# A low-rank sum kept in its four groups of partitions, with two copies of V, and another order of the first loads

## The chip, the cores and the metric

The kernel runs on one core of one Trainium2 chip. The metric is the device time of one execution, in microseconds. The kernel before the change took 668.86 us, the median of three runs (668.37, 668.86 and 669.84).

## What is computed

A lightning attention is followed by a mixer with a low-rank token mix. B = 4, H = 8, S = 768, D = 64, so the model width C = H D is 512; the rank is 32.

```python
# attention, in blocks of 64 positions, state kv per (batch, head)
out[block] = ((q @ k.T) * Dmask) @ v + (q * lam_pow) @ kv
kv = lam**64 * kv + (k * rev_pow).T @ v
# mixer: x is out as (B, S, H*D)
h  = x.transpose(0, 2, 1) @ U @ V          # U: 768 x 32, V: 32 x 768
u  = x + h.transpose(0, 2, 1)
ch = relu(u @ w_ch1) @ w_ch2               # 512 x 2048, 2048 x 512
return u + ch
```

U, V, w_ch1 and w_ch2 arrive as 64-bit floats and are turned into 32-bit ones on the chip.

## The kernel before

The 3072 rows (four batches of 768) are worked on as 24 tiles of 128 rows, NT = 6 tiles to a batch. The kernel has two parts. In the first, some 114 us, the attention of all tiles is computed, and the token mix and the split of u into exact pieces follow seven tiles behind. In the second, TensorE multiplies u with w_ch1 and the result with w_ch2, each product as three passes over pieces of the numbers.

**Pieces of numbers.** TensorE multiplies numbers of the type F32R. Where more precision is wanted, a number is split into a high part (its bits under the mask HI) and the rest, its low part, and the products of the parts are summed. For the token mix all four products of V's two parts and of the low-rank sum's two parts are taken.

**The order.** The first part is written out by hand as a list, `pieces` (line 637 and on), of steps per tile s; each engine runs its instructions in the order of that list. For a step s the list has, in short: `prep(s+1)` (q and k of the next tile transposed by TensorE, copied out by ScalarE, L364, and the next loads of q and k issued on SP), `turn` and `mix` of the tiles seven or eight behind, `next_of_low` at a batch's first tile, `scale(s+1)` on GpSimd (qs, ks), `fade` on ScalarE, `split` and `mixed` on VectorE (L628, L629, L571), `intra` and `state` (px and pkv, L447 and L425), `next_v` (the load of v three tiles on, issued on ScalarE's queue), `inter` (L458 and ScalarE's copy x_nat, L464), `scores(s+1)` (pss, L406) and `masked(s+1)` (sm on VectorE, L415). `aside(s)` puts the conversion of U, V and w_ch1 between these, step by step; a conversion's work on ScalarE is put off to `late`.

**The low-rank sum.** After the last tile of a batch, `low(b)` multiplies x of its six tiles with U on TensorE: 48 matmuls, L474. The sum pp is a PSUM tile of 128 x 128: group g of 32 partitions holds columns 128 g to 128 g + 127 of the 32 x 512 result. The tile takes the bank that px uses otherwise. For batches 0 to 2, `low` then copies groups 0 and 1 to rows 0 to 31 of an SBUF tile on ScalarE (L484), and `low_rows` groups 2 and 3 on VectorE (L516), and masks the 32 x 512 result (L519). In the next step three functions, run by `next_of_low`, fill p_hl, 128 x 512: `spread` casts the high part into all four groups (L527: four instructions, 32 x 256), `low_part` subtracts on GpSimd (L531: two, 32 x 256) and `spread_low` copies the low part into the other two groups (L538: two). `mix(s)`, first run one step later, multiplies:

```python
for low in range(2):
    for x in range(2):
        nc.tensor.matmul(out=pm[:, x], lhsT=weights[half[x]],
            rhs=p_hl[half[x], low * 2 * P : (low + 1) * 2 * P], ...)
```

Here half[x] is 64 of the 128 partitions, and `weights` is a slice of v_hl, which holds V's high part in groups 0 and 2 and its low part in groups 1 and 3. The last batch's sum goes another way (one matmul of 128 rows, L566).

**V.** `v_steps` loads V's 64-bit words in two halves, converts them on VectorE and ScalarE, masks them (L700) and fills v_hl: four casts on ScalarE for the high part (L707), two subtractions on VectorE and two on GpSimd for the low part (L711), each 32 x 384.

**Places.** v_hl and p_hl are two parts of one tile `vp` of the weights' pool, and two constants of the conversion (`set_ends`) lie behind them in it. The row of lam has its own small tile.

**First loads.** Before the first step the loads of q, k, q, k (tile 0 in halves) are issued on SP (q) and ScalarE (k), then v, k, v, q on SP (the third k, the first two v, the third q), U, and the fourth k. The third v is issued on ScalarE's queue after `prep(0)`. Every load of q, k or v of a tile is 256 KB in rows of 256 bytes.

Of the kernel before, what the change touches and what calls it, by code (L numbers as in the profile page):

```python
# [14 lines left out]
P = 128  # L15
# [3 lines left out]
def kernel(  # L19
# [267 lines left out]

    assert G == 4
    vp = w1_pool.tile([P, 3, C], F32R, tag="w1", name="vp").rearrange("p n c -> p (n c)")
    v_hl, p_hl = vp[:, 0:S], vp[:, S : S + C]  # L290


    ident = keep.tile([P, P], FP32, name="ident")
    small = consts.tile([P, 16], FP32, name="small")
    zeros = small[:, 0:1]

    mask = consts.tile([P, 2, HP, P], FP32, name="mask")
# [166 lines left out]
        nc.scalar.copy(xs[s].rearrange("p (a x e) -> p x a e", a=HP, x=2), px)  # L464
        del st[s]

    pps, others = {}, {}

    def low(b):

        pp = two_banks("pp", "px")[:, 0, 0:P] if b < B - 1 else bank([P, P], "pp", "b2")
        for c in range(NT):
            for g in range(G):
                nc.tensor.matmul(  # L474
                    out=pp[g * R : (g + 1) * R, :], lhsT=u_w[:, c, :],
                    rhs=xs[b * NT + c][:, g * P : (g + 1) * P],
                    start=(c == 0), stop=(c == NT - 1),
                )
        if b == B - 1:
            pps[b] = pp  # L480
            return
        pps[b] = rows_f = tmp("p_f")[0:R]
        for g in range(2):
            nc.scalar.copy(rows_f[:, g * P : (g + 1) * P], pp[g * R : (g + 1) * R])  # L484
        others[b] = pp

    def low_rows(b):

        pp, t = pps.pop(b), tmp("p_h")[0:R]
        own = [(slice(g * R, (g + 1) * R), slice(g * P, (g + 1) * P)) for g in range(G)]  # L490
        if b == B - 1:
            h, h2, l, l2 = (p_hl[g * R : (g + 1) * R] for g in range(G))
            for rows, cols in own:
                nc.vector.tensor_scalar(
                    t[:, cols].bitcast(U32), pp[rows].bitcast(U32), HI, None, ALU.bitwise_and
                )

            def low_part():
                for rows, cols in own:
                    nc.vector.tensor_tensor(  # L500
                        out=l[:, cols], in0=pp[rows], in1=t[:, cols], op=ALU.subtract
                    )

            def spread():
                nc.scalar.copy(h, t)
                nc.scalar.copy(h2, t)

            def spread_low():
                nc.scalar.copy(l2, l.bitcast(FP32))

            pps[b] = [spread, low_part, spread_low]
            return

        rows_f, pp = pp, others.pop(b)
        for g in range(2, G):
            nc.vector.tensor_copy(  # L516
                out=rows_f[:, g * P : (g + 1) * P], in_=pp[g * R : (g + 1) * R]
            )
        nc.vector.tensor_scalar(t.bitcast(U32), rows_f.bitcast(U32), HI, None, ALU.bitwise_and)  # L519
# [15 lines left out]

        def spread_low():
            for x in range(2):
                nc.scalar.copy(place(2 * x + 1, 1), place(2 * x, 1).bitcast(FP32))  # L538

        pps[b] = [spread, low_part, spread_low]  # L540

    def next_of_low(b):
        pps[b].pop(0)()
# [7 lines left out]

    def mix(s):
        b, c = divmod(s, NT)
        weights = v_hl[:, c * P : (c + 1) * P]
        if b < B - 1:
            pm = both_halves(s)[:, :, 2 * P :]
            for low in range(2):
                for x in range(2):
                    nc.tensor.matmul(  # L559
                        out=pm[:, x], lhsT=weights[half[x]],  # L560
                        rhs=p_hl[half[x], low * 2 * P : (low + 1) * 2 * P],
                        start=(low == 0), stop=(low == 1),
                    )
            return
        pu = bank([P, C], "pu", "b2")
        nc.tensor.matmul(out=pu, lhsT=weights, rhs=p_hl, start=True, stop=True)  # L566
        nc.vector.tensor_tensor(out=xs[s], in0=pu, in1=xs[s], op=ALU.add)

    def mixed(s):
# [64 lines left out]

    splits = {}

    pieces = [("prep", 0), ("third_v", 0), ("scale", 0), ("scores", 0), ("masked", 0)]
    for s in range(NS):
        b, c = divmod(s, NT)
        done = s - NT - 1  # L640
        more = s + 1 < NS
        turns = done > 0 and (done - 1) // TG < FG
        mixes = 0 <= done < NS - NT - 1
        rows = c == 0 and b > 0
        step = [("prep", s + 1)] * more
        step += [("turn", done - 1)] * turns + [("mix", done)] * mixes
        step += [("mix", done + 1)] * (not more)
        step += [("next_of_low", b - 1)] * rows + [("next_of_low", b - 1)] * rows
        step += [("scale", s + 1)] * more
# [12 lines left out]
        step += [("aside", s)] * (0 < s < NT - 2 or s > NT)  # L662
        step += [("masked", s + 1)] * more
        step += [("low_rows", b)] * (more and c == NT - 1)
        step += [("aside", s)] * (s in (0, NT - 2, NT - 1, NT))
        step += [("store", done)] * (done >= 0 and done // TG < FG)
        pieces += step
    waiting = {name: list(range(NS)) for name in "qkv"}

    def load_next(name, engine=nc.sync):  # L670
# [10 lines left out]
        "third_v": lambda s: load_next("v", nc.scalar), "scale": scale, "turned": lambda s: turned.pop(s)(),  # L681
    }
    def v_steps():

# [7 lines left out]
        def parts(gs):  # L692
            for half in range(2):
                rows, cols = slice(half * R, (half + 1) * R), slice(half * SH, (half + 1) * SH)
                for g in gs:
                    yield v_hl[g * R : (g + 1) * R, cols], rows

        def five():
            st["t"] = t = wconv.tile([P, C], FP32, tag="wt", name="vt")[0 : 2 * R, 0:SH]
# [3 lines left out]
            on_scalar(high)  # L703

        def high():
            for out, rows in parts((0, 2)):
                nc.scalar.copy(out, st["t"][rows])  # L707

        def low(g, engine):
            for out, rows in parts((g,)):  # L710
                engine.tensor_tensor(  # L711
                    out=out, in0=st["v"][rows], in1=st["t"][rows], op=ALU.subtract
                )

        halves = [moe_V[:, half * SH : (half + 1) * SH] for half in range(2)]
        return weight_steps(dst, halves, SH, 2 * R, in_parts=True) + [
            five, lambda: low(1, nc.vector), lambda: low(3, nc.gpsimd),
        ]


# [3 lines left out]
    side = {}  # L724
    for steps, at in (
        (u_side, (-1, 1, 1, 2, 2)),
        (v_steps(), (0, 0, 3, 3, 4, 4, 4, 5, 5)),
        (w1_steps(0, True), (3, 4, 5, 6, 8, 9, 10, 11, 13, 14, 15)),
        (w1_steps(1, True, True), (8, 9, 10, 11, 16, 17, 19, 20, 21, 22, 23, NS)),
    ):  # L730
# [14 lines left out]

    ordered = ctx.enter_context(ExitStack())
    ordered.enter_context(tc.manual_schedule())
    lam_row = consts.tile([1, H + P], FP32, name="lam_row")
    blank = x_pool.tile([P, C], FP32, tag="x", name="blank")[:, 0:P]
    nc.vector.memset(blank, 0.0)  # L750
    nc.vector.memset(lam_row[:, H:], 1.0)
    set_ends(vp[:, S + C : S + C + 2].bitcast(FP32))
# [302 lines left out]
```

## Time and profile before

| What | us |
|---|---|
| median of the runs (3) | 668.86 |
| the profiled execution's own time | 665.92 |
| its span | 664.1 |
| TensorE matmuls busy in the span | 655.3 |
| VectorE busy | 491.0 |
| ScalarE busy | 280.2 |
| GpSimd busy | 115.7 |
| end of the attention's last px (L458) | 113.7 |

The span runs from the first to the last instruction that the profile has; times in the profile count from its start. PE is TensorE's matmuls, PEld its weight loads, DVE VectorE, ACT ScalarE, POOL GpSimd, SP SyncE, which only issues transfers here; a q behind a name is the engine's queue. A row of the timeline has start, length, engine, line, operation, out<-in, and in square brackets the idle time of the engine before it with what ended it. TensorE's ends are modelled, so two of its rows can overlap. "issue" is time in which an engine waited for nothing that the profile shows.

### The profile page before, as it was taken

The numbers are of one execution on the slowest core, as the hardware profiler recorded it, in microseconds if no ns is written. First come the engines' busy times: TensorE is split into PE (matmuls) and PEld (weight loads), VectorE is DVE, ScalarE is ACT, GpSimd is POOL, SyncE is SP. The second block draws the span as 40 slices with busy tenths as digits, with TensorE's granted clock in tenths as the row PEclk, the third lists the DMA queues.
The fourth block names the chain that finished last, engine by engine and source line by source line (L and its number), as shares of the span: only waits on it lengthen the run. The fifth ranks groups of instructions, "written<-read, shape, count | busy, mean of one in ns | idle before, by whom it ended". The sixth has DMA issues, their size and how long they took to land.

```text
span 664.1 us, 13400 instructions
## 1 busy us (share of the span) xinstructions
PE 655.3 (99%) x5242; PEld 538.9 (81%) x5242; DVE 491.0 (74%) x862; ACT 280.2 (42%) x530; POOL 115.7 (17%) x98
## 2 busy tenths in 40 slices
PE   8999999999999999999999999999999999999997
PEld 8888989888888888888888888888888888888886
DVE  5579989969999777777796256786685775775854
ACT  4777886555555444444453122332322322322220
POOL 4466876330000000000000000030120300300300
PEclk9999999999999999999999999999999999999999
DMA  9999982445867655555578899763363363543521
GB/s 225 256 239 248 246 216 96 150 169 171 278 239 255 212 201 203 202 202 204 199 267 290 310 324 399 249 211 106 95 209 104 116 192 95 175 141 96 172 82 63
DMA packets 131776, 131.29 MB, mean 198 GB/s; under 512 B 81346, under 2 KB 89794, under 8 KB 131714
## 3 DMA queue, kind: packets, MB, share of 16 engines
q1 hardware_dynamic: 106592, 124.02, 58.3%
q10 hardware_dynamic: 25122, 6.42, 4.3%
q8 instruction: 41, 0.67, 0.4%
q14 instruction: 21, 0.17, 0.1%
HBM read 80.09 MB, written 50.33 MB: 196 GB/s over the span
## 4 chain that ended last, share of the span: by engine, by line
PE 94%; DMA 2%; DVE 1%; SPq 1%; ACT 1%; issue 1%; POOL 0%; ACTq 0%; DVEq 0%
PE pz L818 27%; PE pz L953 14%; PE pz L951 14%; PE pd L828 14%; PE pd L955 13%; PE px L447 3%; PE pss L406 3%; PE px L458 2%; PE pqk L358 2%; PE pkv L425 1%; SPq L279 1%; DMA kraw<-in_k_dram 1%; PE pp L474 1%; DMA qraw<-in_q_dram 1%; PE pm L559 1%; PE put L590 1%
## 5 line engine op out<-in xcount | busy, mean ns | idle before, releaser
L818 PE MATMUL pz<-u_hl,w 128*128 128x512 f32 x768 | 190.1, 398 | 0.0
L818 PEld LDWEIGHTS pz<-u_hl,w 128*128 128x128 f32 x768 | 144.2, 189 | 35.0 <-ACT r L824 0.3
L953 PE MATMUL pz<-w_hl,m 128*128 128x512 f32 x384 | 151.1, 397 | 0.0
L951 PE MATMUL pz<-w_hl,m 128*128 128x512 f32 x384 | 151.0, 397 | 0.0
L955 PE MATMUL pd<-w_d,m 128*128 128x512 f32 x384 | 149.5, 397 | 0.0
L934 ACT ACTIVATE m<-mt 128x512 fp32r<-128x512 f32 x96 | 60.6, 632 | 196.8 <-PE pd L955 137.8
L935 DVE SCALAR_TENSOR_TENSOR m<-rm,m 128x512 fp32r<-128x512 f32 x96 | 71.4, 746 | 52.5 <-ACT m L934 52.2
L980 POOL TENSOR_TENSOR o<-o,u 128x512 f32<-128x512 f32 x20 | 29.8, 1522 | 447.4 <-DVE o L976 447.4
L833 DVE SCALAR_TENSOR_TENSOR r<-pd,r 128x512 f32<-128x512 f32 x96 | 61.8, 686 | 53.3 <-ACT r L824 43.5
L828 PE MATMUL pd<-u_d,w 128*128 128x512 f32 x384 | 98.6, 397 | 0.0
L824 ACT ACTIVATE r<-pz 128x512 f32<-128x512 f32 x96 | 52.1, 596 | 92.7 <-PE pz L818 92.6
L953 PEld LDWEIGHTS pz<-w_hl,m 128*128 128x128 f32 x384 | 72.4, 189 | 17.6
L951 PEld LDWEIGHTS pz<-w_hl,m 128*128 128x128 f32 x384 | 72.4, 188 | 17.6
L955 PEld LDWEIGHTS pd<-w_d,m 128*128 128x128 f32 x384 | 72.4, 189 | 17.5
L828 PEld LDWEIGHTS pd<-u_d,w 128*128 128x128 f32 x384 | 72.2, 189 | 17.2
L936 DVE SCALAR_TENSOR_TENSOR m<-m 128x512 fp32r<-128x512 f32 x96 | 69.0, 721 | 0.9
L933 DVE TENSOR_SCALAR mt<-rm 128x512 uint32<-128x512 uint32 x96 | 46.1, 481 | 28.5 <-DMA rm<-r_d 28.2
L415 DVE TENSOR_TENSOR sm<-pss,mask 128x512 f32<-128x512 f32 x48 | 30.9, 684 | 8.0 <-PE pss L406 7.6
L212 ACT CAST w<-wt 128x512 fp32r<-128x512 f32 x32 | 19.9, 620 | 30.6 <-DVE wt L209 23.4
L447 PE MATMUL px<-vraw,sm 128*64 128x64 f32 x768 | 27.9, 225 | 2.4 <-ACT x_nat L464 0.7
L447 PEld LDWEIGHTS px<-vraw,sm 128*64 128x64 f32 x768 | 25.0, 138 | 5.4 <-ACT qt L364 1.8
L406 PE MATMUL pss<-qt,kt 64*128 64x128 f32 x384 | 28.9, 291 | 0.0
(96 smaller groups left out, 667.7 us busy)
## 6 DMA issues: line engine op xcount, KB each, us to landing
r_d<-r SPq DMA_DIRECT2D x96, 256.0 KB, 2.4
rm<-r_d SPq DMA_DIRECT2D x96, 256.0 KB, 2.7
words<-in_moe_w_ch_dram SPq DMA_DIRECT2D x30, 512.0 KB, 4.4
w_d<-w SPq DMA_DIRECT2D x16, 768.0 KB, 3.4
w_hl<-w_d SPq DMA_DIRECT2D x16, 512.0 KB, 6.3
u_d<-x_nat SPq DMA_DIRECT2D x24, 256.0 KB, 3.9
u<-u_d SPq DMA_DIRECT2D x24, 256.0 KB, 4.1
qraw<-in_q_dram SPq DMA_DIRECT2D x23, 256.0 KB, 4.2
```

The costliest lines, as they stand in the source:

```text
L406: nc.tensor.matmul(out=pss[:, x, a, :], lhsT=kt[half[x], a, :], rhs=qt[half[x], a, :], start=True, stop=True,)
L447: nc.tensor.matmul(out=px[half[t], x, a, :], lhsT=sm[:, x, a, half[t]], rhs=vr[:, 2 * a + x, :], start=(a == 0), stop=(alone and a == HP - 1),
L818: nc.tensor.matmul(out=acc[g][0], lhsT=w[:, n, ct, :], rhs=uhl[g][:, n, ct, :], start=(ct == 0 and n == 0), stop=(ct == CT - 1 and n == 1),)
L824: nc.scalar.mul(rs[g], acc[g][0], 4096.0 + 1.0)
L828: nc.tensor.matmul(out=acc[g][1], lhsT=w[:, 2, ct, :], rhs=ud[g][:, ct, :], start=(ct == 0), stop=(ct == CT - 1),)
L833: nc.vector.scalar_tensor_tensor(rs[g], acc[g][1], 4096.0, rs[g], ALU.mult, ALU.add)
L934: nc.scalar.activation(out=m[:, 0], in_=t, func=AF.Relu)
L935: nc.vector.scalar_tensor_tensor(m[:, 1], r, 0.0, hi, ALU.max, ALU.subtract)
L936: nc.vector.scalar_tensor_tensor(m[:, 2], hi, E, low, ALU.mult, ALU.subtract)
L951: nc.tensor.matmul(out=pz, lhsT=m[:, 0, cols], rhs=hl[:, 0], start=first, stop=False)
L953: nc.tensor.matmul(out=pz, lhsT=m[:, 1, cols], rhs=hl[:, 1], start=False, stop=end)
L955: nc.tensor.matmul(out=pd, lhsT=m[:, 2, cols], rhs=dd, start=first, stop=end)
```

## The change

The low-rank sum stays in its four groups. VectorE copies the whole 128 x 128 tile to SBUF and masks it there; ScalarE casts each group's high part (four, 32 x 128), and GpSimd subtracts each group's low part (four, 32 x 128), into a p_hl of 128 x 256. A half x of its partitions holds, in its first 32, the high part of columns 256 x to 256 x + 255, and in its second 32 their low part. The four products then need V twice: once with its high part in groups 0 and 2 and its low part in 1 and 3, and once the other way round. v_hl becomes 128 x 2 x 768. The conversion fills only group 0 (high, ScalarE) and group 1 (low, GpSimd) of the first copy, and six transfers inside SBUF, 32 x 768 each, issued on SP at the start of step 6 (`spread_v`), fill the other six places. The first mix is in step 7.

Each mix is still four matmuls over 64 partitions and 256 columns. The last batch's four parts lie in the second copy of V, which is no longer needed then.

v_hl fills `vp`; p_hl becomes a tile of its own, the row of lam moves into the tile of `blank` (zeros), and the two constants into `small`.

In the first loads, v, k, v, q becomes v, k, q, k; U comes after that. The second v is issued on ScalarE's queue after `prep(0)` and the third after `prep(1)`.

```diff
-    v_hl, p_hl = vp[:, 0:S], vp[:, S : S + C]
+    v_hl = vp.rearrange("p (n c) -> p n c", n=2)
+    p_hl = consts.tile([P, 2 * P], F32R, name="p_hl")
...
     def low(b):
...
-        pps[b] = rows_f = tmp("p_f")[0:R]
-        for g in range(2):
-            nc.scalar.copy(rows_f[:, g * P : (g + 1) * P], pp[g * R : (g + 1) * R])
-        others[b] = pp
+        pps[b] = pp
...
     def low_rows(b):
...
-        rows_f, pp = pp, others.pop(b)
-        for g in range(2, G):
-            nc.vector.tensor_copy(
-                out=rows_f[:, g * P : (g + 1) * P], in_=pp[g * R : (g + 1) * R]
-            )
-        nc.vector.tensor_scalar(t.bitcast(U32), rows_f.bitcast(U32), HI, None, ALU.bitwise_and)
-        wide = [slice(x * 2 * P, (x + 1) * 2 * P) for x in range(2)]
+        whole, t = tmp("p_f")[:, 0:P], tmp("p_h")[:, 0:P]
+        nc.vector.tensor_copy(out=whole, in_=pp)
+        nc.vector.tensor_scalar(t.bitcast(U32), whole.bitcast(U32), HI, None, ALU.bitwise_and)
 
         def place(g, low):
-            return p_hl[g * R : (g + 1) * R, wide[low]]
-
-        def spread():
+            n = 2 * (g // 2) + low
+            return p_hl[n * R : (n + 1) * R, (g % 2) * P : (g % 2 + 1) * P]
+
+        def high_part():
             for g in range(G):
-                nc.scalar.copy(place(g, 0), t[:, wide[g // 2]])
+                nc.scalar.copy(place(g, 0), t[g * R : (g + 1) * R])
 
         def low_part():
-            for x in range(2):
+            for g in range(G):
+                rows = slice(g * R, (g + 1) * R)
                 nc.gpsimd.tensor_tensor(
-                    out=place(2 * x, 1), in0=rows_f[:, wide[x]], in1=t[:, wide[x]],
-                    op=ALU.subtract,
-                )
-
-        def spread_low():
-            for x in range(2):
-                nc.scalar.copy(place(2 * x + 1, 1), place(2 * x, 1).bitcast(FP32))
-
-        pps[b] = [spread, low_part, spread_low]
+                    out=place(g, 1), in0=whole[rows], in1=t[rows], op=ALU.subtract
+                )
+
+        pps[b] = [high_part, low_part]
...
     def mix(s):
-        weights = v_hl[:, c * P : (c + 1) * P]
+        weights = v_hl[:, :, c * P : (c + 1) * P]
...
-            for low in range(2):
+            for n in range(2):
                 for x in range(2):
                     nc.tensor.matmul(
-                        out=pm[:, x], lhsT=weights[half[x]],
-                        rhs=p_hl[half[x], low * 2 * P : (low + 1) * 2 * P],
-                        start=(low == 0), stop=(low == 1),
+                        out=pm[:, x], lhsT=weights[half[x], n], rhs=p_hl[half[x]],
+                        start=(n == 0), stop=(n == 1),
                     )
...
-        step = [("prep", s + 1)] * more
-        step += [("turn", done - 1)] * turns + [("mix", done)] * mixes
+        step = [("spread_v", s)] * (s == NT) + [("prep", s + 1)] * more
+        step += [("another_v", s)] * (s == 0) + [("turn", done - 1)] * turns + [("mix", done)] * mixes
...
-        step += [("next_of_low", b - 1)] * rows
...
     def v_steps():
...
-            for out, rows in parts((0, 2)):
+            for out, rows in parts(0):
                 nc.scalar.copy(out, st["t"][rows])
 
-        def low(g, engine):
-            for out, rows in parts((g,)):
-                engine.tensor_tensor(
+        def low():
+            for out, rows in parts(1):
+                nc.gpsimd.tensor_tensor(
                     out=out, in0=st["v"][rows], in1=st["t"][rows], op=ALU.subtract
                 )
 
+        def spread():
+            whole = v_hl.bitcast(FP32)
+            for g, n in ((2, 0), (1, 1), (3, 1), (3, 0), (0, 1), (2, 1)):
+                source = (g + n) % 2
+                nc.sync.dma_start(
+                    out=whole[g * R : (g + 1) * R, n],
+                    in_=whole[source * R : (source + 1) * R, 0],
+                )
...
-    for name in "vkvq":
+    for name in "vkqk":
         load_next(name)
     aside(-1)
-    load_next("k")
```

More of the change, by code (lines that the diff above doesn't have):

```diff
@@ L289 @@
     vp = w1_pool.tile([P, 3, C], F32R, tag="w1", name="vp").rearrange("p n c -> p (n c)")
-    v_hl, p_hl = vp[:, 0:S], vp[:, S : S + C]
+    v_hl = vp.rearrange("p (n c) -> p n c", n=2)
+    p_hl = consts.tile([P, 2 * P], F32R, name="p_hl")
     ident = keep.tile([P, P], FP32, name="ident")
-    small = consts.tile([P, 16], FP32, name="small")
+    small = consts.tile([P, 18], FP32, name="small")
     zeros = small[:, 0:1]
@@ L465, in inter @@
         del st[s]
-    pps, others = {}, {}
+    pps = {}
     def low(b):
@@ L481, in low @@
             return
-        pps[b] = rows_f = tmp("p_f")[0:R]
-        for g in range(2):
-            nc.scalar.copy(rows_f[:, g * P : (g + 1) * P], pp[g * R : (g + 1) * R])
-        others[b] = pp
+        pps[b] = pp
     def low_rows(b):
-        pp, t = pps.pop(b), tmp("p_h")[0:R]
+        pp = pps.pop(b)
         own = [(slice(g * R, (g + 1) * R), slice(g * P, (g + 1) * P)) for g in range(G)]
         if b == B - 1:
-            h, h2, l, l2 = (p_hl[g * R : (g + 1) * R] for g in range(G))
+            t = tmp("p_h")[0:R]
+            h, h2, l, l2 = (v_hl[g * R : (g + 1) * R, 1, 0:C] for g in range(G))
             for rows, cols in own:
@@ L565, in mix @@
         pu = bank([P, C], "pu", "b2")
-        nc.tensor.matmul(out=pu, lhsT=weights, rhs=p_hl, start=True, stop=True)
+        nc.tensor.matmul(out=pu, lhsT=weights[:, 0], rhs=v_hl[:, 1, 0:C], start=True, stop=True)
         nc.vector.tensor_tensor(out=xs[s], in0=pu, in1=xs[s], op=ALU.add)
@@ L635 @@
     splits = {}
-    pieces = [("prep", 0), ("third_v", 0), ("scale", 0), ("scores", 0), ("masked", 0)]
+    pieces = [("prep", 0), ("another_v", 0), ("scale", 0), ("scores", 0), ("masked", 0)]
     for s in range(NS):
@@ L679 @@
         "mixed": mixed, "store": store, "next_v": next_v, "split": lambda s: splits.pop(s)(),
-        "third_v": lambda s: load_next("v", nc.scalar), "scale": scale, "turned": lambda s: turned.pop(s)(),
+        "another_v": lambda s: load_next("v", nc.scalar), "scale": scale, "turned": lambda s: turned.pop(s)(),
     }
@@ L690, in dst, with parts @@
             return st["v"]
-        def parts(gs):
+        def parts(g):
             for half in range(2):
                 rows, cols = slice(half * R, (half + 1) * R), slice(half * SH, (half + 1) * SH)
-                for g in gs:
-                    yield v_hl[g * R : (g + 1) * R, cols], rows
+                yield v_hl[g * R : (g + 1) * R, 0, cols], rows
         def five():
@@ L705, in high @@
         def high():
-            for out, rows in parts((0, 2)):
+            for out, rows in parts(0):
                 nc.scalar.copy(out, st["t"][rows])
-        def low(g, engine):
-            for out, rows in parts((g,)):
-                engine.tensor_tensor(
+        def low():
+            for out, rows in parts(1):
+                nc.gpsimd.tensor_tensor(
                     out=out, in0=st["v"][rows], in1=st["t"][rows], op=ALU.subtract
                 )
+        def spread():
[6 more added lines that the diff above has]
+                )
+        run["spread_v"] = lambda s: spread()
         halves = [moe_V[:, half * SH : (half + 1) * SH] for half in range(2)]
         return weight_steps(dst, halves, SH, 2 * R, in_parts=True) + [
-            five, lambda: low(1, nc.vector), lambda: low(3, nc.gpsimd),
+            five, low,
         ]
@@ L726 @@
         (u_side, (-1, 1, 1, 2, 2)),
-        (v_steps(), (0, 0, 3, 3, 4, 4, 4, 5, 5)),
+        (v_steps(), (0, 0, 3, 3, 4, 4, 4, 5)),
         (w1_steps(0, True), (3, 4, 5, 6, 8, 9, 10, 11, 13, 14, 15)),
@@ L747 @@
     ordered.enter_context(tc.manual_schedule())
-    lam_row = consts.tile([1, H + P], FP32, name="lam_row")
-    blank = x_pool.tile([P, C], FP32, tag="x", name="blank")[:, 0:P]
+    blank = x_pool.tile([P, C], FP32, tag="x", name="blank")
+    lam_row, blank = blank[0:1, P : P + H + P], blank[:, 0:P]
     nc.vector.memset(blank, 0.0)
     nc.vector.memset(lam_row[:, H:], 1.0)
-    set_ends(vp[:, S + C : S + C + 2].bitcast(FP32))
+    set_ends(small[:, 16:18])
     nc.scalar.dma_start(out=lam_row[:, 0:H], in_=lam.unsqueeze(0))
```

## The prediction

> **What bounds the kernel now.** I read the engine shares first, then busy time by stretches, then the chain that ended last, then the timeline wherever that chain leaves TensorE. In the busy times by stretch the first four numbers after the width are TensorE's matmuls, its weight loads, VectorE and ScalarE:
>
> ```profile
> 0.00:30.00 30.00, 26.83 (x588) 24.40 (x588) 16.90 (x46) 16.50 (x41) 14.23 (x18) 1.00 1.03 235
> 30.00:60.00 30.00, 28.86 (x794) 26.33 (x796) 24.56 (x44) 22.52 (x54) 19.50 (x17) 1.00 1.03 251
> 60.00:90.00 30.00, 29.50 (x824) 27.03 (x822) 27.16 (x47) 23.01 (x55) 22.16 (x19) 1.00 0.97 244
> 140.00:400.00 260.00, 260.00 (x1111) 209.14 (x1110) 192.95 (x346) 117.64 (x204) 2.60 (x2) 1.00 0.68 236
> ```
>
> From 115 us on TensorE has no gap until the last stores. So a microsecond won before that should reach the end whole, and only some 5 us can be won: 3.2, 1.1 and 0.5 us idle in these stretches and 0.3 up to 115. The change touches four places there. The first is in the timeline:
>
> ```profile
> 12.33 0.47 PE L358 MATMUL pqk<-ident,qraw 64*128 64x64 f32 x8 [0.91 <-DMA qraw<-in_q_dram]
> ```
>
> The third q arrives at 12.19 and TensorE has waited 0.91 us. The second place is the first use of the low-rank product, in the chain (start, length, what):
>
> ```profile
> 38.60 0.49 PE pqk L358 x16
> 39.09 0.18 PE pm L559 x2
> 39.27 0.39 ACT vp L538
> 39.66 0.02 issue
> 39.69 0.59 ACT x_nat L464
> 40.28 0.04 issue
> 40.33 1.15 PE px L447 x32
> ```
>
> ScalarE is late. The four copies of V (L707, 2.07 us), two of the product (L484, 0.52), four of its high part (L527, 1.66) and two of its low part (L538, 0.83) stand in its queue between 32.5 and 39.7, and the evacuation L464 that frees the px bank is behind them. The other two places are the next batch boundaries, alike:
>
> ```profile
> 62.26 0.67 PE pqk L358 x16
> 62.92 0.01 issue
> 62.94 0.28 DVE p_f L516
> 63.22 0.01 issue
> 63.24 0.30 DVE p_f L516
> 63.54 0.02 issue
> 63.56 0.41 DVE p_h L519
> 63.98 0.03 issue
> 64.01 0.70 DVE ut L628
> 64.71 0.02 issue
> 64.73 0.69 DVE u_hl L629
> ```
>
> Here the product occupies the px bank until VectorE's second copy ends (63.54), and px starts at 63.63. The VectorE row that follows (ut, u_hl, x_nat, kv) ends at 66.36, and the next pqk shares kv's bank.
>
> **What the skill says.** *DMA: Bandwidth & Descriptors*, "Issuing engines are not separate DMA queues": SP and ScalarE feed the same 16 DMA engines. The trace agrees: a DMA share of 1.03 with both queues in use. So moving v to ScalarE's queue reorders the loads; it makes no bandwidth. The same page, "Anatomy of one DMA", has about 2.0 us fixed cost per transfer, mostly the write's receipt, fitted on another path. The shortest landing of a q load here is 2.4 us, so I use 2.0 as the floor for the new copies. *SBUF — State Buffer*, "SBUF: two separate sides", has an exclusive lock between VectorE (two SBUF inputs) and GpSimd. The trace agrees: L531 takes 1.02 us beside VectorE's L711 and 0.72 without it.
>
> **The change, part by part.**
>
> *Matrix products.* Eighteen mixes of four matmuls, [64 x 128] by 256 columns, before and after. 0.
>
> *Product rows (low, low_rows, three boundaries).* Removed from each: ScalarE 2 x 0.256 (L484) + 4 x 0.403 (L527) + 2 x 0.403 (L538) = 2.93 us. Added: four casts 32x128. The casts take 403, 510 and 618 ns for 256, 384 and 512 columns, so 0.84 ns a column and 296 ns for 128: 1.18 us. ScalarE saves 1.75 us. VectorE drops 2 x 0.288 + 0.414 and gains one 128x128 copy from PSUM (0.288, the row of equal width) and one mask of 128 columns (192 columns take 0.25, 384 take 0.35, so 0.22): it saves 0.48 us and no longer waits for ScalarE's two copies. GpSimd: two at 0.726 become four; 512 columns take 1.28, so 2.16 ns a column and 0.45 us each: +0.35 us. This is covered: its qs is used 2.1 us after it is ready (67.02 against 69.14). Without that cover it would be 0.35 us a boundary.
>
> At 62.26: copy to 62.6, mask to 62.85, ut from the turn's end at 63.2 instead of 64.01. The px bank is free at 62.6, so px follows the mix after 0.41 us, as in other steps, not 0.66: 0.25. From pss to pqk it is 0.99 us in other steps and 1.23 here (65.18 to 66.41): 0.24. Kv then ends near 65.7, before pqk wants its bank at 65.9. Gain 0.49; at the third boundary 0.19 + 0.24 = 0.43. Together 0.9 us.
>
> *V's parts.* VectorE loses 2 x 0.767, ScalarE 2 x 0.51. GpSimd keeps two at 1.0 us. In their place SP issues six copies inside SBUF, 32 rows x 3 KB, at the head of step 6, past the loads of q and k behind them. SP is free then: its next load waits for TensorE from 33.5 to 35.73. The first copies wait for ScalarE's two casts (33.55) and the others for GpSimd (34.26). But the trace has eight semaphores for transfers, used about in turn, and an issue waits until the transfer before it on its semaphore has landed. If the six take them in turn, the fifth waits for a q load that landed at 35.37 and the sixth for a k load at 37.04. The DMA engines were nearly idle then:
>
> ```profile
> 36.00:37.00 1.00, 1.00 (x38) 1.00 (x40) 0.95 (x3) 0.95 (x2) 0.65 (x1) 1.00 0.24 66
> ```
>
> So the first five flow at once, and the sixth lands at about 37.1 + 2.0 = 39.1. No row shows such a copy. From below: no semaphore wait, all landed by 38, before the mix at 38.9 needs them. From above: 6.4 us, the longest landing of a k load in this trace, so 43.5. I take 39.1: the engines have little else to do. The last matmul of the mix then ends near 39.4 and px starts at 39.45 instead of 40.33: gain 0.9. With no late copy it is px at 39.3 (the mix's 0.41 after 38.89): 1.0. With 43.5 it is a loss of 3.5. ScalarE has x_nat done by 39.0 and doesn't decide. The q, k and weight loads behind the six come about 1.5 us later; q of tile 10 lands by 42.5 and is read at 47. V's load on ScalarE stays ahead of x_nat. If its semaphore were the sixth copy's, x_nat would end at 39.8 and 0.4 of the gain would go.
>
> *Order of the first loads.* Third q takes the second v's place in SP's queue (landed 11.29), the second v takes the third v's on ScalarE (issued 6.36, landed 10.71), and the third v goes after the second tile's copies, at about 9.4. TensorE is ready for q at 11.42, so up to 0.9 us is won there; the second v is needed at 12.1. But the bytes up to the fourth q are the same set, at 235 GB/s and full engines, and it landed at 15.95 with TensorE ready at 16.05. At 21 us DMA decides once more: ScalarE's issue of the sixth v (21.13) waits for the semaphore of a k load that lands at 21.05, and the x_nat of tile 2 is queued behind it. I expect 0.3 us to be left at 22 us. What is left only brings TensorE earlier to the mix, which waits for the sixth copy: 0 to 0.9 from below and above, taken as 0.
>
> *Small moves* (lam_row into blank's tile, ends into small, k's fourth load ahead of U): no instruction more, a few load places; 0.
>
> **Sum.** 0.9 (first mix) + 0.9 (two boundaries) + 0 = 1.8 us. The profiled execution ran 665.92 us with a span of 664.1, so it would be 664.1 with a span of 662.3. It lies 2.9 below the median of the runs, 668.86, and I take the difference off that: 667.1. A measurement of this kernel can tell about 0.2%, 1.3 us, from no change.
>
> **Rivals.**
> (1) All cover holds: the copies land before the mix wants them and 0.9 of the order of loads survives. 1.0 + 0.9 + 0.9 = 2.8, so 666.1. For it: the DMA gap at 36 us. Against it: full DMA engines until 35.
> (2) The copies or a semaphore wait on ScalarE eat the gain at the first mix, and only the boundaries are left: 0.9, so 668.0, within 0.2%. For it: each of the six is one more link in SP's order.
> (3) Slower: the sixth copy lands late. One place, the mix of tile 0. It decides once the landing passes 42.3 (px then at 42.6, 2.3 us lost against 0.9 won). At 43.5, with px at 43.8, it costs 3.5 - 0.9 = 2.6: 671.5. For it: landings of 5.2 us in the middle and 6.4 at most on the same queue. Against it: those were in full queues.
> (4) The load order does nothing, since DMA is full: already in my sum.
>
> **How the numbers follow.** Forecast 0.42, (1) 0.13, (2) 0.31 with shifts to zero or a little above, (3) 0.14, of which 0.02 stays inside 0.2%. Faster 0.55, same 0.33, slower 0.12. The range, 665.7 to 669.9, holds (1), the forecast and (2) with the spread of the runs (about 0.7 either side), and leaves out most of (3). The forecast's own range is 666.4 to 667.6.
>
> **What would show it.** L484 and L538 gone; px of tile 7 at 39.3 to 39.8; pqk 0.99 us after pss at both later boundaries; six SBUF copies on SP between 33.5 and 37.5, the last landing near 39; no wait of TensorE for q at 12 us. I am wrong if the mix of tile 0 waits for a DMA beyond 40, if a ScalarE load waits for a copy's semaphore, or if GpSimd's four subtractions end after the next mix wants them.

## The result and the profile after

The changed kernel took 670.78 us, the median of seven runs (669.61 to 672.07). The kernel before, run beside it, took 669.15 (666.65 to 670.21). The ratio is 1.0031, with a 95% interval of 1.0015 to 1.0047: slower by 1 to 3 us, where 1.8 us less was forecast. The profiled execution ran 669.61 us with a span of 667.7; that of before ran 665.92 with 664.1.

The busy times by stretch after the change, in the columns of before (start and end, width, TensorE's matmuls, weight loads, VectorE, ScalarE, GpSimd, granted clock, DMA share, GB/s):

```profile
0.00:30.00 30.00, 27.78 (x595) 25.40 (x596) 17.07 (x46) 16.51 (x41) 14.21 (x18) 1.00 1.05 239
30.00:60.00 30.00, 28.17 (x724) 25.69 (x720) 20.25 (x37) 18.89 (x46) 17.53 (x18) 0.94 0.97 241
...
```

From 60 us on the clock is 1.00 as before. In the first stretch TensorE is busy 0.95 us longer than before. ScalarE, at 22.52 us in the second, is down to 18.89, in part simply because the stretch holds less of the work (724 matmuls where it held 794). The new number is the clock of the second stretch: 0.94, where it was 1.00. A slower clock makes TensorE busier for the same work, so the matmul column alone hides it.

TensorE's timeline at the first use of the product, tile 0's mix in step 7:

```profile
38.03 0.36 PE L551 MATMUL pm<-p_hl,vp 64*128 64x256 f32 x1
38.90 0.35 PE L551 MATMUL pm<-p_hl,vp 64*128 64x256 f32 x1 [0.51 <-ACT qt L365]
40.45 0.53 PE L551 MATMUL pm<-p_hl,vp 64*128 64x256 f32 x2 [1.20 <-DMA vp<-vp]
40.90 1.52 PE L448 MATMUL px<-vraw,sm 128*64 128x64 f32 x32
```

The mix could start at 38.03, but its matmuls come one by one, as the copies land, and the last two only at 40.45. (The profile puts the second one's wait down to ScalarE's qt, which the mix does not read; that matmul needs the fourth copy, which landed at 38.65.) So px starts at 40.90; it was 40.33 before, and 39.45 was forecast. TensorE does almost nothing for 2.2 us. And px then takes 1.52 us for the work that took 1.15 before.

Why it takes longer stands in the columns of the same view by single microseconds:

```profile
39.00:40.00 1.00, 0.25 (x1) 0.05 (x1) 0.07 (x1) 0.97 (x4) 1.00 (x2) 1.00 0.68 209
40.00:41.00 1.00, 0.56 (x4) 0.46 (x6) 0.00 (x0) 0.48 (x3) 0.49 (x1) 1.00 1.07 243
41.00:42.00 1.00, 1.00 (x29) 1.00 (x31) 0.69 (x1) 0.00 (x0) 0.00 (x0) 0.75 1.11 260
42.00:43.00 1.00, 1.00 (x24) 1.00 (x22) 0.00 (x0) 0.00 (x0) 0.00 (x0) 0.50 0.91 227
43.00:44.00 1.00, 1.00 (x34) 0.88 (x34) 0.42 (x1) 0.00 (x0) 0.64 (x1) 0.50 1.24 289
44.00:45.00 1.00, 1.00 (x23) 0.88 (x17) 0.00 (x0) 0.59 (x1) 0.42 (x1) 0.55 1.08 287
```

The column after GpSimd is the granted clock. It falls to one half in the 42nd microsecond and comes back in the 45th: 0.25 + 0.5 + 0.5 + 0.45 = 1.7 us of clock lost, or 3.4 us at half speed. The chain that ended last shows what stands ahead of it:

```profile
30.51 6.37 DMA kraw<-in_k_dram
36.88 0.01 issue
36.90 3.42 DMA vp<-vp
40.31 0.14 issue
40.45 0.53 PE pm L551 x2
40.97 1.45 PE px L448 x32
```

The load of k that was issued at 30.51 lands at 36.88 and releases the issue of a copy, which takes 3.42 us to land; and that copy is the fifth, not the sixth. All six, as one group of instructions (nanoseconds of an issue, least, middle and most; first and last start; then the time from issue to landing, of the five copies whose landing can be told):

```profile
L708 SPq DMA_DIRECT2D vp<-vp x6: 537/589/659, 33.7 to 37.6; - x6
DMA to landing us min/median/max: 2.9/3.3/3.7
```

The sixth is issued at 37.60 and lands at 40.48.

At the third batch boundary the row that holds the px bank is one copy of 128x128 and one mask of 128 columns, as worked out:

```profile
92.10 0.29 DVE L514 COPY p_f<-pp 128x128 f32<-128x128 f32 x1 [0.18 <-PE pp L475]
92.50 0.23 DVE L515 TENSOR_SCALAR p_h<-p_f 128x128 uint32<-128x128 uint32 x1
...
93.35 2.00 POOL L528 TENSOR_TENSOR p_hl<-p_f,p_h 32x128 fp32r<-32x128 f32 x4 [1.20 <-PE pm L551]
```

px (93.15) follows the mix (92.74) after 0.41 us. I compare the steps by the times at which the scores (pss) of a tile start on TensorE:

| Start of the scores of tile | 7 | 9 | 12 | 14 | 18 | 20 | 23 | end of span |
|---|---|---|---|---|---|---|---|---|
| before | 37.43 | 46.84 | 59.65 | 69.77 | 86.91 | 96.97 | 109.88 | 664.1 |
| after | 36.57 | 48.86 | 61.80 | 72.26 | 89.42 | 99.12 | 112.94 | 667.7 |

The changed kernel is 0.86 us ahead at tile 7 and 2.02 behind at tile 9: 2.9 us went in two steps. The 0.86 is mostly not the change's work: 0.52 of it is a pause in the execution of before, at 35.43, that the profile puts down to "issue". The third boundary (18 to 20) takes 9.70 us in place of 10.06. The second (12 to 14) takes 10.46 in place of 10.12, with a pause of 0.67 us in its px that the profile puts down to "issue". Between tiles 20 and 23 another 0.91 us is lost, which I did not settle. From tile 23 to the end it is 554.8 in place of 554.2. That last half microsecond and the pauses are taken up below.

### The profile page after: what moved, and what is told of

Read it like the earlier page. It is cut to its first block, busy times and chain, and to the rows that moved or that the text cites. A ratio compares the mean times of both kernels' runs of the same rounds, so it can differ in the third digit from the quotient of the medians.

```text
span 667.7 us, 13403 instructions
## 1 busy us (share of the span) xinstructions
PE 658.0 (99%) x5242; PEld 541.1 (81%) x5242; DVE 488.1 (73%) x857; ACT 273.9 (41%) x516; POOL 116.0 (17%) x104
## 4 chain that ended last, share of the span: by engine, by line
PE 97%; DMA 1%; issue 0%; ACT 0%; SPq 0%; DVE 0%; DVEq 0%; ACTq 0%
PE pz L816 27%; PE pz L951 13%; PE pd L826 13%; PE pz L949 13%; PE pd L953 13%; PE pss L407 4%; PE px L448 4%; PE px L459 2%; PE pqk L359 2%; PE pkv L426 2%; DMA kraw<-in_k_dram 1%; PE pm L551 1%; PE pp L475 1%; PE pm L599 1%; PE put L581 1%; DMA vp<-vp 1%
```

## The experiments

The theory I formed from these lines: the copies land late, TensorE idles, its clock is halved for 3.4 us, and these two together are the loss. The rivals: the new order of the first loads, the number of copies in SP's queue, or something later in the run. Experiments of one batch share a chip and the runs of the kernel before, so the 667.07, 666.84 and 666.88 below are three such batches. The diffs are shortened.

**TensorE kept busy while it waits.** Eight matmuls on zeros (their result is used by nothing) stand ahead of tile 0's mix:

```diff
+        step += [("busy", s)] * (s == NT + 1)      # keep_busy(8)
         step += [("turn", done - 1)] * turns + [("mix", done)] * mixes
```

> The changed kernel, with eight matmuls on zeros (128 x 128, result unused) ahead of the mix of tile 0, so that TensorE works while it would wait for the copies of V. Theory A (the late copies stall TensorE, and the idle time lets its granted clock fall to half): px of tile 7 starts where it does in the changed kernel (41.0 us, within 0.4), the granted clock stays at 1.00 from 41 to 45 us, and the run is 1.2 to 1.8 us shorter than the changed kernel: ratio to before 1.000 to 1.001. Rival B (the new order of the first loads costs the time): nothing changes, ratio 1.002 to 1.004. Rival C (the fall of the clock has another cause than the idle time): clock and ratio as in the changed kernel.

Measured: 668.14 us (14 runs) against 667.07; ratio 1.0008, interval 0.9990 to 1.0026. TensorE's timeline of this kernel:

```profile
37.73 2.05 PE L344 MATMUL idle<-blank 128*128 128x128 f32 x16
41.03 0.72 PE L551 MATMUL pm<-p_hl,vp 64*128 64x256 f32 x3 [0.75 <-DMA vp<-vp]
41.68 1.15 PE L448 MATMUL px<-vraw,sm 128*64 128x64 f32 x32
```

(The eight matmuls are 16 instructions in the trace.) Here the copies landed even later, the last at 41.26, and px starts at 41.68, later than expected (41.0, to within 0.4). But it takes 1.15 us, the clock is 1.00 in every microsecond from 41 to 45, and all 14 runs have a mean clock of 0.998 or more. From this px to the scores of tile 9 it is 6.47 us; in the kernel before it is 6.51 and in the changed one 7.96. So the halved clock costs 1.45 us where it happens, and keeping TensorE at work removes it although the copies are no earlier. The trace shows this, the times do not: the changed kernel was not run in this batch, and the interval here overlaps those of its two measurements (1.0015 to 1.0047 above, 1.0010 to 1.0041 below).

**One copy instead of six.** The engines fill two groups of both copies of V, and one transfer of 64 partitions fills the rest (one more pair of casts on ScalarE, one more pair of subtractions, on VectorE):

```diff
-            for g, n in ((2, 0), (1, 1), (3, 1), (3, 0), (0, 1), (2, 1)):
-                source = (g + n) % 2
-                nc.sync.dma_start(out=whole[g * R : (g + 1) * R, n], in_=whole[source * R : (source + 1) * R, 0])
+            nc.sync.dma_start(out=whole[2 * R :], in_=whole[0 : 2 * R])
```

> The changed kernel with the first two groups of both copies of V filled by the engines (ScalarE four casts instead of two, VectorE two subtractions more, GpSimd two as it was) and one transfer of 64 partitions by 6 KB in place of the six. Theory A: it is issued by 34.5 us and lands by 38.2, px of tile 7 starts at 38.3 to 39.2 instead of 41.0, the clock stays at 1.00, and the run is 3 to 4 us shorter than the changed kernel: ratio to before 0.996 to 0.999. Rival B: px of tile 7 earlier, but a ratio of 1.002 or more. If this copy lands only at 40, the clock falls again and the ratio stays near 1.003.

Measured: 667.20 us (22 runs) against 667.07; ratio 0.9996, interval 0.9982 to 1.0010. The single copy is issued at 34.98 and lands at 39.74, after 4.8 us; 38.2 was expected:

```profile
39.88 0.47 PE L551 MATMUL pm<-p_hl,vp 64*128 64x256 f32 x3 [1.71 <-DMA vp<-vp]
40.27 1.29 PE L448 MATMUL px<-vraw,sm 128*64 128x64 f32 x32
```

In this execution the clock fell as well (0.57 to 0.50 from 41 to 44), and from px to the scores of tile 9 it is again 7.96 us. The runs differ: the four with a mean clock of 0.997 took 668.5 us in the middle (one with 0.996 took 669.6), the six with 0.998 took 667.6, and the five with 0.999 and the six with 1.000 took 666.0 and 667.0. So one copy does not always escape the drop. The time met neither expectation: not the 0.996 to 0.999 of a copy that lands by 38.2, nor the 1.003 of one that lands at 40.

**The load order alone**, in the kernel before:

```diff
-    for name in "vkvq":
+    for name in "vkqk":
         load_next(name)
     aside(-1)
-    load_next("k")
...
+        step += [("third_v", s)] * (s == 0)        # load_next("v") on ScalarE's queue
```

> The kernel before with the new order of the first loads alone (v, k, q, k on SP; second and third v on ScalarE's queue). Theory A: TensorE's wait for q at 12 us goes, scores of tile 3 start up to 0.3 us earlier, and little is left: ratio 0.9985 to 1.0005. Rival B: ratio 1.002 to 1.004.

Measured: 666.83 us (22 runs) against 667.07; ratio 0.9993, interval 0.9981 to 1.0005. No loss, and no gain that can be told. TensorE's wait for q at 12 us is gone, but the scores of tile 3 start at 19.43, where it was 19.40.

**The changed kernel with the old load order:**

```diff
-    for name in "vkqk":
+    for name in "vkvq":
         load_next(name)
     aside(-1)
+    load_next("k")
...
-        step += [("another_v", s)] * (s == 0)
```

> The changed kernel with the order of the first loads as before the change. Theory A: the sixth copy still lands after 40 us, TensorE waits and its clock falls; ratio to before 1.002 to 1.004. Rival B: the loss is gone, ratio 0.997 to 1.000.

Measured: 668.95 us (22 runs) against 667.07; ratio 1.0028, interval 1.0013 to 1.0043. As slow as the changed kernel. In its profiled execution the whole chain is later: copies issued from 36.32 to 40.22, the last landing at 42.66, and TensorE's wait longer:

```profile
42.54 0.81 PE L551 MATMUL pm<-p_hl,vp 64*128 64x256 f32 x3 [2.90 <-DMA vp<-vp]
```

Its clock falls at 41.48 and stays at one half for 6.8 us, twice as long as in the changed kernel. The wait alone costs time too: the seven runs with a mean clock of 0.999 or 1.000 took 668.6 us in the middle. So the order of the loads is not the cause of the loss.

**The first mix later in its step.** If the copies' lateness is all, TensorE should be given other work until they land. Tile 0's mix goes behind the second px of tile 7, and what VectorE does with its result goes behind with it:

```diff
-        ... [("mix", done)] * mixes
+        ... [("mix", done)] * (mixes and done > 0)
...
         step += [("next_v", s), ("inter", s)]
+        step += [("mix", done)] * (done == 0)
...
-        step += [("mixed", done)] * mixes
+        step += [("mixed", done)] * (mixes and done > 0)
...
         step += [("low", b)] * (more and c == NT - 1)
+        step += [("mixed", done)] * (done == 0)
```

> The changed kernel with the mix of tile 0 put later in the step, behind inter(7) and ahead of scores(8), so that TensorE has px, pkv and the second px of tile 7 to do while the copies land. Late copies and the clock that falls behind them as the cause: the copies land near 40.5 and the mix wants them near 41, TensorE is not idle for 2 us, the granted clock stays at 1.00 from 41 to 45, px of tile 7 starts at 38.3 to 39.2, and the kernel is 3 to 3.8 us shorter than the changed kernel: ratio to before 0.996 to 0.999. If the loss comes from something later in the run: ratio 1.001 to 1.004, as the changed kernel.

Measured: 664.60 us (8 runs) against 666.84; ratio 0.9966, interval 0.9951 to 0.9980. The timeline of this kernel:

```profile
38.66 1.24 PE L448 MATMUL px<-vraw,sm 128*64 128x64 f32 x32 [0.35 <-issue]
40.92 0.51 PE L551 MATMUL pm<-p_hl,vp 64*128 64x256 f32 x4
41.26 1.05 PE L407 MATMUL pss<-qt,kt 64*128 64x128 f32 x16
```

The copies land no earlier (the last at 40.78), but the mix wants them at 40.92, only just later: its four matmuls run in one row with no wait, px has already run at 38.66, and the clock is 1.00 from 37 to 46. The scores of tile 9 start at 45.45, 1.39 us earlier than in the kernel before and 3.41 earlier than in the changed one. (Of the 1.39, 0.77 were there at the scores of tile 7 already, mostly the pause in the execution of before.) The changed kernel, run in the same batch, took 668.81 us, and no run of it was as short as the longest of these eight.

**The later mix with the product's rows gathered as before** (two copies each on ScalarE and VectorE into 32 partitions, a mask of 512 columns, then two casts and two subtractions of 256 columns into the new p_hl):

```diff
-        whole, t = tmp("p_f")[:, 0:P], tmp("p_h")[:, 0:P]
-        nc.vector.tensor_copy(out=whole, in_=pp)
+        for g in range(2): nc.scalar.copy(rows_f[:, g * P : (g + 1) * P], pp[g * R : (g + 1) * R])
+        for g in range(2, G): nc.vector.tensor_copy(out=rows_f[:, g * P : (g + 1) * P], in_=pp[g * R : (g + 1) * R])
...
-            for g in range(G): nc.scalar.copy(place(g, 0), t[g * R : (g + 1) * R])
+            for x in range(2): nc.scalar.copy(place(x, 0), t[:, wide[x]])
```

> The same, with the low-rank product's rows gathered in 32 partitions as before the change (ScalarE two and VectorE two copies, a mask of 512 columns, two casts of 256 columns, two subtractions on GpSimd of 256 columns). If the gain at the two batch boundaries belongs to the split in four groups: each boundary 0.36 to 0.44 us longer than in the kernel with the later mix, 0.8 us over the whole, ratio 0.001 above that one. If the gain has another cause: the same time as that one.

Measured: 666.25 us (14 runs), ratio 0.9998, interval 0.9982 to 1.0015. The boundaries give the cleaner reading: the second takes 10.12 us and the third 10.06, exactly as in the kernel before, and 9.69 each with the split in four groups. That part of the change is worth 0.43 + 0.37 = 0.80 us. The medians stand 1.65 us apart, which their intervals allow but the boundaries do not explain.

**The kernel before with the same later mix** (the same diff):

> The kernel before, with the mix of tile 0 put later in the same way. If ScalarE's lateness at the first mix is what the later place removes, px of tile 7 starts at 39.3 instead of 40.33 and the kernel gains up to 1.0 us: ratio 0.9985 to 1. If the gain of the later place needs the change: ratio 1.

Measured: 667.34 us (14 runs), ratio 1.0014, interval 1.0000 to 1.0028.

```profile
39.44 1.15 PE L447 MATMUL px<-vraw,sm 128*64 128x64 f32 x32 [1.18 <-ACT x_nat L464]
```

px starts at 39.44, near the 39.3 that was expected, but not for the expected reason: this execution was 0.83 us ahead at the scores of tile 7 (36.60 against 37.43). Counted from there px comes after 2.84 us, where it was 2.90, because it still waits for ScalarE, which has its four casts for V and the product's copies in its queue; and the mix now comes behind it, so the scores of tile 8 come after 5.45 us, where it was 5.12. The later place alone gains nothing. That what it uses is the room on ScalarE that the change makes fits this wait, but was not tested apart.

**The changed kernel again**, on the same chip:

> The changed kernel itself, to be compared on the same chip: ratio 1.002 to 1.004, granted clock 0.995 to 0.997 in every run, px of tile 7 near 40.9 and the clock at half for some 3 us after it.

Measured: 668.81 us (10 runs) against 666.84; ratio 1.0025, interval 1.0010 to 1.0041. The expectation had the clock drop in every run. It was in seven, with a mean clock of 0.996 or 0.997 and 668.6 to 669.3 us in the middle. Three had 0.999: two of them took 666.2 and 666.6, no more than the kernel before, the third 668.8; and one of the seven took 667.05. So the time goes with the clock, by some 2 us, but not run by run, and the clock does not always fall. In the profiled execution it falls at 40.64, for 3.4 us again, and px starts at 41.22. There the fourth copy is the late one: its issue took 1.82 us and it landed at 40.10. (The profile puts TensorE's wait of 2.01 us down to GpSimd's qs, which the mix does not read.) In six of the eight traces with six copies one of the issues took 1.2 to 1.8 us; what held it is not shown.

**Two transfers more.** The last half microsecond: in the kernels with six copies the span ends 3.3 us after VectorE's last operation, in those without copies 2.8. SP's last instructions wait in a fixed order for eight transfer semaphores. In the kernel before the last two stores are on semaphores 105 and 106, second and third in that order. With six more transfers they are on 102 and 104, the last store on the one that is asked for first; all other waits then follow its landing, and in each such trace there is a pause of some 0.3 us between two of them. So I split two later loads in halves, which makes the six transfers more into eight:

```diff
-            nc.sync.dma_start(out=us[n], in_=u_d[g * TG + n])
+            halves = [slice(0, C // 2), slice(C // 2, C)] if g == 0 and n < 2 else [slice(0, C)]
+            for part in halves:
+                nc.sync.dma_start(out=us[n][:, part], in_=u_d[g * TG + n][:, part])
```

> The kernel with the later mix, with two loads of the second part (u of tiles 0 and 1 of the first group) split in halves, so that the program has eight transfers more than the kernel before instead of six. In all six kernels profiled with the six copies the span ends 3.3 us after VectorE's last operation, in the three without them 2.8: the last stores' semaphores come first instead of third in SP's closing row of waits. If that is the cause: the stores are back on the semaphores they have in the kernel before, and the span ends 2.8 to 2.9 us after VectorE's last operation, 0.5 us shorter than with the later mix alone (too little for the times alone: ratio to before about 0.996 against 0.9966). If the 0.5 us belongs to the copies in another way: 3.3 us as with the later mix.

The timeline's head and VectorE's last operation in this kernel:

```profile
core 0 of [0], span 662.3 us
...
658.61 0.75 DVE L978 SCALAR_TENSOR_TENSOR o<-pd,o 128x256 f32<-128x256 f32 x2
```

From 659.36 to 662.3 it is 2.9 us; with the later mix alone it was 3.3 (658.77 to 662.1). So 0.4 us is back, with the stores again on 105 and 106. The order of the waits is not all of it: the kernel with one copy, whose stores are on 106 and 107, has 3.4, with the same pause behind the waits; why the pause comes is not shown. The time, 665.25 us (9 runs) against 666.88, ratio 0.9977, interval 0.9959 to 0.9996, is too coarse to show that.

**One copy, later mix and two split loads** together:

> The kernel with one copy of 64 partitions instead of six of 32 (the engines fill two groups of both copies of V), with the later mix, and the two split loads. If a copy that lands before the mix wants it costs nothing, and the six copies cost nothing beyond that either: the copy lands near 39.7, the mix starts near 41 without a wait, clock 1.00, and the time is that of the kernel with the later mix within 1 us, ratio 0.995 to 0.998. If SP's four us of issues held up the loads behind them: 0.5 to 1 us shorter than the kernel with the later mix and two more transfers. Both stores at the end on later semaphores: span ends 2.6 to 3.0 us after VectorE's last operation.

Measured: 665.61 us (14 runs), ratio 0.9980, interval 0.9966 to 0.9994. The copy is issued at 36.19 in this execution and lands at 40.90; the mix starts at 42.30 without a wait. The last stores are on 108 and 109, and the span ends 3.0 us after VectorE's last operation, as expected. It is no faster than six copies: once the mix does not wait for them, SP's four us of issues cost nothing that can be told.

**The later mix once more**, beside the last two:

> The kernel with the later mix again, to be compared on the same chip: ratio 0.995 to 0.998, granted clock 0.998 to 1, span ending 3.3 us after VectorE's last operation.

Measured: 665.64 us (22 runs) against 666.88; ratio 0.9979, interval 0.9970 to 0.9989, every run with a clock of 0.998 or more. By its two measurements the kernel with the later mix beats the kernel before by 0.2 to 0.3%, and the changed one by 0.6% in the batch that has both.

One step of all traces, side by side, free of what each execution gained or lost before it:

| From the scores of tile 7 to those of tile 9 | us |
|---|---|
| before | 9.41 |
| before, new load order | 9.41 |
| before, later mix | 10.03 |
| changed (two traces) | 12.29, 12.39 |
| changed, TensorE kept busy | 12.01 |
| changed, old load order | 14.13 |
| changed, one copy | 11.89 |
| later mix (two traces) | 8.79, 8.93 |
| later mix, rows gathered | 8.80 |
| later mix, two transfers more | 8.79 |
| later mix, one copy | 9.14 |

## Why the prediction was wrong, step by step

**The first mix (forecast: gain 0.9; it lost 2.0 in the trace).** Two steps failed.

The first is "the sixth lands at about 37.1 + 2.0 = 39.1". The mechanism was there: an issue held until a k load landed at 36.88. Three terms were short. The load's semaphore held the fifth copy, since a load of v had taken a turn between, so a whole issue followed. An issue takes 0.54 to 0.66 us, and I had given it nothing. And a landing takes 2.9 to 3.7 us. The 2.0 us of the Trainium skill (*DMA: Bandwidth & Descriptors*, "Anatomy of one DMA") was fitted on another path; I used it as a floor and then took the floor for the value, since the engines were "nearly idle". That held for one microsecond, 36 to 37; the next two of the trace of before have a DMA share of 1.04 and 1.20. How much of a landing is the queue's and how much the copy's own is not shown: the first of the six, too, took 3.7 us. The sum is 37.60 + 2.88 = 40.48. For px that is 1.45 us, 40.90 in place of 39.45. This is rival (3)'s mechanism at less than its size.

The second is rival (3)'s point of decision: "once the landing passes 42.3". It priced each us of TensorE's wait at one us. By that price px at 40.90 is 0.57 us worse than before, which the boundaries pay for, and the kernel would still have been a little faster. The halved clock added 1.45 us, and neither a step nor a rival had it. The Trainium skill has the effect: *TensorE: Matmul & The Clock Gate*, "What's actually happening", gives half the clock after an idle window of about 3.4 us, and full clock after about as long at work. The second number is what this trace shows (3.4 us at half). The first is not: here the clock fell after 3.4 us in which TensorE was busy for half of the time. The same section calls the window free-running, and the traces agree: the clock changes only on a grid of 3.41 us that does not follow the waits (last section). That in the three runs with a mean clock of 0.999 the pause lay across two stretches of the grid would fit; none of them was profiled.

**The two boundaries (forecast 0.49 + 0.43).** Right: 0.43 and 0.37 by the kernel with the rows gathered again. The prices behind them were right too: copy 0.29 (0.288), mask 0.23 (0.22), cast 0.296 (0.296), GpSimd 0.45 each (0.45). In the changed kernel's own trace the second boundary shows no gain because of the 0.67 us "issue" pause. Such pauses of 0.3 to 1.6 us stand at other places in each execution, that of before included. What causes them stays open.

**The order of the first loads (forecast: 0.3 us ahead at 22 us, worth nothing).** That it is worth nothing was right: alone it changes nothing that can be told. In the two traces TensorE is 0.33 us ahead at the scores of tile 6 (31.58 against 31.91), but over all traces that time lies anywhere from 30.68 to 32.52, with either order, so the 0.3 is not confirmed. TensorE's wait for the third q at 12 us is gone, as expected.

**ScalarE at the first mix.** Right: L484 and L538 are gone, no load on its queue waited for a copy's semaphore, and with the later mix px starts at 38.66.

**Edits costed at nothing.** With six transfers more the last stores fell on other semaphores of SP's closing row of waits, and the end came 0.4 to 0.5 us later. I had looked at the copies' own semaphores and not at who comes after them in turn.

With the measured terms the sum is 0.57 (px at 40.90 against 40.33) + 1.45 (clock) + 0.5 (end) - 0.8 (boundaries) = +1.7 us. The medians say +1.6, the ratio +1.0 to +3.1. With the mix later it is -1.39 (scores of tile 9) - 0.8 + 0.5 = -1.7, and the two ratios say -2.3 and -1.4. Both sums take the times as one execution of each kernel has them. Counted from the scores of tile 7 (the table above) they are 2.88 + 0.5 - 0.8 = +2.6 and -0.62 - 0.8 + 0.5 = -0.9, so they are good to about one microsecond.

## What to carry to other kernels

A copy that feeds TensorE should be priced from its issue, with the issues ahead of it and a landing that such a copy was seen to take, not a floor. If TensorE would stand still for a microsecond or two, price the clock as well as the wait, and look for independent matmuls to put ahead of the instruction that waits: moving one mix some 3 us back in TensorE's order turned a loss of 0.3% into a gain of 0.2 to 0.3%. And read the clock column by single microseconds around each new wait, since a halved clock looks like a busy engine.

## What the runs showed of the hardware

TensorE's clock changes on a grid. By the traces' records of the clock, the times between its changes inside a run are whole multiples of 3.413 us in all thirteen traces: in the changed kernel it rises at 10.77, falls at 41.49 (nine stretches later) and comes back at 44.90. Every fall before the end of a run followed a stretch of this grid in which TensorE's matmuls were busy for half of the time or less:

| Kernel | Stretch of the grid | Busy share | Clock after it |
|---|---|---|---|
| changed | 38.08 to 41.49 | 0.50 | 0.5 |
| changed, second trace | 37.23 to 40.64 | 0.41 | 0.5 |
| changed, one copy | 37.73 to 41.14 | 0.50 | 0.5 |
| changed, old load order | 38.06 to 41.48 | 0.46 | 0.5 |
| the same, next stretch, at half clock | 41.48 to 44.89 | 0.69 | 0.5 |
| later mix, second trace | 74.45 to 77.86 | 0.54 | 1.0 |
| before, later mix | 36.87 to 40.28 | 0.65 | 1.0 |
| changed, TensorE kept busy | 37.38 to 40.79 | 0.81 | 1.0 |

So a fall lasted one stretch (3.4 us), or two where the stretch after it was not full either. The busy share is not the whole rule: in the last microseconds of the second trace of the later mix a stretch with 0.45 left the clock alone. Eight matmuls on zeros were enough to keep it in the trace, and judged by a mean of 0.997 or less, the clock fell in seven of ten runs of the changed kernel in one batch and in all seven in another.

A copy of 96 KB inside SBUF landed 2.3 to 4.5 us after its issue in all kernels here, one of four times the bytes in 4.7 to 4.8. Counted from VectorE's last operation, the program ended 0.5 us later with six transfers more and 0.1 later with eight more; the semaphores on which the last stores fell went with it.
